# Weight unpacking, carried gate columns and half of the score mask moved from VectorE to ScalarE and GpSimd in a chunked delta-rule attention with a gated MoE

## The chip, the cores and the metric

The kernel runs on one core of one Trainium2 chip. A core has five engines that each run their own instructions in order and meet through semaphores: TensorE (PE, with its weight loads as PEld), VectorE (DVE), ScalarE (ACT), GpSimd (POOL) and SyncE (SP, which here only starts transfers). The metric is the device time of one launch in microseconds, lower is better. A change is given as the median of several runs against runs of the kernel before.

## What is computed

An attention with a decaying state, corrected by a delta rule, over 768 tokens, for 4 batches and 8 heads of width 40; then its output (4, 768, 320) goes through a linear layer to 1024 columns, a convolution of three tokens per column, a sigmoid gate and a linear layer back to 320.

```python
for t in range(S):                      # attention, state (B, H, 40, 40)
    y[:, :, t] = einsum('bhd,bhde->bhe', rt, state)
    Sa = einsum('bhde,bhe->bhd', state, at)
    state = state * wt - einsum('bhd,bhe->bhde', Sa, bt) + einsum('bhd,bhe->bhde', vt, kt)
...
h = maximum(x @ w_in, 0)                # x: (B, S, 320)
conv_out[s] = conv_w[0] * h[s-1] + conv_w[1] * h[s] + conv_w[2] * h[s+1]
out = (h / (1 + exp(-conv_out))) @ w_out
```

The inputs come as 64-bit floats; the attention's inputs are converted ahead, the three weight arrays are read by the kernel as pairs of 32-bit words.

## The kernel before

**Attention.** The 768 tokens are 24 chunks of 32. Within a chunk the recurrence is a triangular system, so that a chunk needs one inverse, and the state (four tiles of 120x360, one per batch) moves once per chunk. Two chunks make a pair j (12 pairs). Per pair: `decays` and `decayed` (scans and products with the decay, on DVE), `scores` (L421 to L440: products of the decayed rows on PE into a bank `ps` of 128x512, half for k and half for b, masked by a strict triangle on DVE into `at`), `solve_in` (the b half of `at` goes out to memory and back, turned, as `bb`), `solve` (L469: 31 steps of two operations each, L480 and L486, then the result goes out and back as `tt`). The inverse of even pairs is worked out on DVE and that of odd pairs on POOL (`VSOL`). Per chunk: `chain` (L505: `psb` on ACT, `pu` on PE from `tt` and `psb`, `u` on ACT, then the new state `pn` on PE, an addition L562 on DVE, four products with the decay L568 on POOL), the turns (`rt`, `vt`, `ut`, `sn`: PE transposes copied by ACT), `pairs` and `outputs` (`pm`, `ms`, `py`, `ysb`) and `finish` (`xf` on DVE, and its two parts `xh` by ACT and `xl` by POOL).

**Weights.** 23 pieces: twelve of w_in (`wi<g><q>`, 120x256: g is a third of the 320 rows, q a quarter of the 1024 columns), the conv weights (`cv`, 24x128), eight of w_out (`wo0` to `wo7`, 128x256) and two with its rest (`wp0`, `wp1`). Each is loaded as 64-bit words, turned into 32-bit floats on DVE by `from_f64` (L213 to L236, eight operations), copied by ACT to the high part (L253, `wih`, `woh`), and the difference is put by POOL into the low part (L255, `wil`, `wol`). The pieces' buffers come from a pool of eight (`gh` and `gl`, four each), so that the first operation on a later piece waits until the last reader of an earlier one is through. The conv piece ends in a PE transpose `pc` (L269).

**Gate.** 12 windows of 64 tokens, each in four groups fp of two times 128 columns. `moe_in` (L687): products into a bank `ph`, relu by ACT into `hb` (L714), whose first two token columns are carried over from the window before: `he`, a part of `hend`, is copied into `hb` (L712) before the relu, and the last two columns go from `hb` to `he` (L716) after it, 128x16 elements each. Then `cc`: the middle tap on ACT (L721), the two outer taps on DVE (L729), sigmoid on ACT (L734), the gate product on DVE (L736), and the split into `g..h` (ACT, L740) and `g..l` (POOL, L743). `moe_out` multiplies by w_out.

**Order.** All work is written as generators with steps (`yield`), and the string `ORDER` says token by token which generator runs one step next: `we7` is a step of weight piece 7, `so1` a stretch of the inverse of pair 1, `ch2` a step of the chain of chunk 2, `mi0.1` one of `moe_in` of window 0, group 1. Every engine runs its instructions in the order in which the steps give them out. A step of a weight piece holds a whole `from_f64`; within `solve` a step ends at i in (4, 8, 12, 16, 20, 24, 28).

Of the kernel before, what the change touches and what calls it, by code (L numbers as in the profile page):

```python
# [8 lines left out]
F32 = mybir.dt.float32  # L9
# [3 lines left out]
AF = mybir.ActivationFunctionType  # L13
ALU = mybir.AluOpType
# [3 lines left out]
C = 32  # L18
# [94 lines left out]
def tile_decay_delta_attention_then_conv_gate_moe(  # L113
# [13 lines left out]
    nc = tc.nc  # L127
    B, H, S, D = r.shape
# [5 lines left out]
    W = WS * C  # L134
# [7 lines left out]
    cp = ctx.enter_context(tc.tile_pool(name="cp", bufs=1))  # L142
# [9 lines left out]
    def bank(shape, name):  # L152
        return psS.tile(shape, F32, tag="S", name=name)

    def buf(pool, shape, tag, name, dt=F32):
        return pool.tile(shape, dt, tag=tag, bufs=BUFS[tag], name=name)

    def quad(i):
        return slice(C * i, C * i + C)
# [7 lines left out]
        out=hmask, in_=hmask, compare_op=ALU.is_ge, fill=0.0,  # L167
# [3 lines left out]
        out=hmask, in_=hmask, compare_op=ALU.is_ge, fill=0.0,  # L171
        base=D - 1, pattern=[[D, 3]], channel_multiplier=-1,
    )
    tri = cp.tile([128, C], F32, name="tri")
    nc.gpsimd.memset(tri, 1.0)
    for q in range(B):
        nc.gpsimd.affine_select(
            out=tri[quad(q), :], in_=tri[quad(q), :],
            compare_op=ALU.is_ge, fill=0.0,
            base=-1, pattern=[[1, C]], channel_multiplier=-1,  # L180
        )
    trin = cp.tile([128, 2, 1, C], F32, name="trin")
    nc.vector.tensor_copy(trin[:, 0, 0], tri)
    nc.vector.tensor_scalar(
        out=trin[:, 1, 0], in0=tri, scalar1=-1.0, scalar2=None, op0=ALU.mult
    )
    xini = cp.tile([128, HS, C], BF16, name="xini")
    nc.gpsimd.memset(xini, 1.0)
    for z in range(2):
        zs = slice(z * 64, z * 64 + 64)  # L190
        nc.gpsimd.affine_select(
            out=xini[zs], in_=xini[zs], compare_op=ALU.is_equal, fill=0.0,
# [20 lines left out]
    def from_f64(raw, e, t, m):  # L213

        lo, hi = raw[..., 0], raw[..., 1]
        V = nc.vector
        V.tensor_scalar(
            out=e, in0=hi, scalar1=20, scalar2=0x7FF,
            op0=ALU.logical_shift_right, op1=ALU.bitwise_and,
        )  # L220
        V.tensor_scalar(
            out=t, in0=hi, scalar1=3, scalar2=0x3FFFFFFF,
            op0=ALU.logical_shift_left, op1=ALU.bitwise_and,
        )
        V.scalar_tensor_tensor(
            out=t, in0=hi, scalar=-(1 << 30), in1=t, op0=ALU.bitwise_and, op1=ALU.bitwise_or
        )
        V.tensor_scalar(out=m, in0=lo, scalar1=8, scalar2=None, op0=ALU.logical_shift_right)
        tf, ef = t.bitcast(F32), e.bitcast(F32)
        V.scalar_tensor_tensor(out=tf, in0=e, scalar=896.5, in1=tf, op0=ALU.is_ge, op1=ALU.mult)  # L230
        V.tensor_scalar(out=e, in0=t, scalar1=-(1 << 23), scalar2=None, op0=ALU.bitwise_and)
        V.scalar_tensor_tensor(
            out=ef, in0=m, scalar=2.0**-44, in1=ef, op0=ALU.mult, op1=ALU.mult
        )
        V.tensor_tensor(tf, tf, ef, ALU.add)
        return tf  # L236

    def words(nm):
# [5 lines left out]
    def piece(nm, load, dsth, dstl, rows, shape):  # L244
        raw, e, t, m = words(nm)
        raw = raw[:rows]
        load(raw)
        yield
        f = from_f64(raw.rearrange("p (c z) -> p c z", z=2), e[:rows], t[:rows], m[:rows])
        if len(shape) == 2:  # L250
            f = f.rearrange("p (a c) -> p a c", a=shape[0])
        yield
        nc.scalar.copy(dsth, f)  # L253
        yield
        nc.gpsimd.tensor_tensor(dstl, f, dsth.bitcast(F32), ALU.subtract)  # L255
        yield

    def conv_piece():
        NCV = KW * NF
        craw, ce, ct, cm = words("cv")  # L260
        nc.sync.dma_start(craw[:NCV, :256], conv_w.rearrange("k (f p) -> (k f) p", p=256))
        yield
        cf = from_f64(
            craw[:NCV, :256].rearrange("p (c z) -> p c z", z=2),
            ce[:NCV, :128], ct[:NCV, :128], cm[:NCV, :128],
        )
        yield
        pc = psM.tile([128, 512], F32, tag="M", name="pc")
        nc.tensor.transpose(pc[:, :NCV], cf, ident[:NCV, :NCV])  # L269
        nc.scalar.copy(cw.rearrange("p k f -> p (k f)"), pc[:, :NCV])  # L270
        yield
        yield
# [132 lines left out]
    def against(ps, x, lhs, mk, first):  # L405

        for g in range(G):
            lo, hi = GH[g]
            h0 = (0, 3, 6)[g]
            for bi in range(B):  # L410
                nc.tensor.matmul(
                    ps[quad(bi), x, h0 : h0 + hi - lo, :], lhs[:, g, quad(bi)],
                    mk[:, g, lo:hi, quad(bi)],
                    start=(first and g == 0), stop=True, skip_group_check=True,
                )

    def gbt(t):
        return t.rearrange("p g b t -> p g (b t)")


    def scores(st):  # L421
        n, c, pd = st["n"], st["c"], st["pd"]
        ah = gbt(pd["ah"][:, c])
        ap = buf(wn, [GR, G, 3, BC], "ap", f"ap{n}")
        for h in range(3):
            g1 = 2 if h == 0 else 3
            nc.scalar.activation(  # L427
                out=ap[:, :g1, h, :], in_=ah[:, :g1], func=AF.Copy, scale=hmask[:, h : h + 1]
            )
        yield  # L430
        if c == 0:
            pd["at"] = buf(wn, [128, 2, 2, H, C], "at", f"at{n}")
        at = pd["at"]
        ps = bank([128, 2, H, C], f"ps{n}")
        for x, nm in enumerate("kb"):
            against(ps, x, gbt(pd[nm + "t"][:, c]), ap, x == 0)
        nc.vector.tensor_tensor(
            at[:, c], ps, trin.to_broadcast([128, 2, H, C]), ALU.mult,
        )
        yield  # L440

# [245 lines left out]
    def moe_in(wd, fp):  # L687
        wi, n = wd["n"], wd["n"]
        xh, xl, xp = wd["xh"], wd["xl"], wd["xp"]
        passes = (  # L690
            (wih[:, 0], xh[:, 0]), (wih[:, 1], xh[:, 1]), (wih[:, 2], xh[:, 2]),
            (wil[:, 0], xh[:, 0]), (wih[:, 0], xl[:, 0]), (wih[:, 1], xl[:, 1]),
            (wil[:, 1], xp), (wil[:, 2], xl[:, 2]),
        )
        ph = psM.tile([128, FP, B, W], F32, tag="M", name=f"ph{n}{fp}")
        for j in range(FP):
            f = FP * fp + j
            fs = slice(f * 128, (f + 1) * 128)
            for i, (l, x) in enumerate(passes):
                nc.tensor.matmul(  # L700
                    ph[:, j], l[:, fs], x,
                    start=(j == 0 and i == 0), stop=(i == len(passes) - 1),
                    skip_group_check=True,
                )
            if j == 0:
                yield
                hb = buf(mo, [128, FP, B, W + 2], "hb", f"hb{n}{fp}")
                he = hend[:, FP * fp : FP * fp + FP]
                if wi == 0:
                    nc.gpsimd.memset(hb[:, :, :, 0:2], 0.0)  # L710
                else:
                    nc.vector.tensor_copy(hb[:, :, :, 0:2], he)  # L712
                yield
        nc.scalar.activation(out=hb[:, :, :, 2 : W + 2], in_=ph, func=AF.Relu)  # L714
        yield
        nc.vector.tensor_copy(he, hb[:, :, :, W : W + 2])  # L716
        yield
        cc = buf(mo, [128, FP, B, W], "cc", f"cc{n}{fp}")
        for j in range(FP):
            f = FP * fp + j  # L720
            nc.scalar.activation(  # L721
                out=cc[:, j], in_=hb[:, j, :, 1 : W + 1], func=AF.Copy,
                scale=cw[:, 1, f : f + 1],
            )
        yield
        for j in range(FP):
            f = FP * fp + j
            for x in (0, 2):
                nc.vector.scalar_tensor_tensor(  # L729
                    out=cc[:, j], in0=hb[:, j, :, x : W + x], scalar=cw[:, x, f : f + 1],  # L730
                    in1=cc[:, j], op0=ALU.mult, op1=ALU.add,
                )
        yield
        nc.scalar.activation(out=cc, in_=cc, func=AF.Sigmoid)  # L734
        yield
        nc.vector.tensor_tensor(cc, cc, hb[:, :, :, 1 : W + 1], ALU.mult)  # L736
        yield
        c2 = cc.rearrange("p j b t -> p (j b t)")
        gh = gp.tile([128, 512], F32R, tag="gh", name=f"g{n}{fp}h")
        nc.scalar.copy(gh, c2)  # L740
        yield
        gl = gp.tile([128, 512], F32R, tag="gl", name=f"g{n}{fp}l")
        nc.gpsimd.tensor_tensor(gl, c2, gh.bitcast(F32), ALU.subtract)  # L743
        wd["gs"][fp] = [t.rearrange("p (j b t) -> p j b t", j=FP, b=B) for t in (gh, gl)]
        yield
# [137 lines left out]
    for st in sts:  # L883
        n, j, c = st["n"], st["n"] // 2, st["c"]
# [118 lines left out]
```

## Time and profile before

| | |
|---|---|
| median of 3 runs | 711.65 us (707.79 to 715.09) |
| the profiled execution | 708.08 us, of it 706.4 span |
| mean granted TensorE clock | 0.906 |
| PE busy | 560.7 us, 79% of the span |
| DVE busy | 538.4 us, 76% |
| ACT busy | 350.7 us, 50% |
| POOL busy | 353.2 us, 50% |

The table's lower part is the first part of the profile page; the span is the time from the first to the last instruction, and 1.7 us of the profiled execution lie around it. Busy shares over the whole span mix two stages: up to some 200 us weights and the first six or seven chunks, after that chunks and windows together. In the rows below, a name such as `wi12q` is the tile of that piece, an L number is the line of the kernel before, an arrow in brackets names what the engine waited for; "x23" counts instructions.

### The profile page before, as it was taken

The page shows a single profiled execution, that of the slowest core. Times are in us where ns is not written, and L with a number is a line of the kernel's source. Part 1 is how long each engine was busy: PE and PEld are TensorE (multiplying, and loading weights), DVE is VectorE, ACT ScalarE, POOL GpSimd, SP SyncE. Part 2 cuts the span into 40 slices and gives each one's busy share as a digit, 9 for nine tenths or more (in the row PEclk, how much of TensorE's full clock was granted, in tenths as well). Part 3 has the DMA queues.
Part 4 walks back from the last instruction along what each step waited for, and adds up shares of the span by engine and source line. Part 5 has one row for each costly group of instructions (what it writes and reads, how often), then busy time and mean ns, then how long its engine had stood idle before and what let it go on. Part 6 is the DMA issues. An engine that isn't in the chain of part 4 may idle for free. (4 is left out here: it accounts for less than half of the span.)

```text
span 706.4 us, 29930 instructions
## 1 busy us (share of the span) xinstructions
PE 560.7 (79%) x13021; PEld 497.9 (70%) x13021; DVE 538.4 (76%) x1261; ACT 350.7 (50%) x792; POOL 353.2 (50%) x582
## 2 busy tenths in 40 slices
PE   4444764677687898988977996899998977899886
PEld 3334654566576787977866885789887876788775
DVE  6689889998999896657795578987979894456571
ACT  2322244254375455664454664466565546455651
POOL 2001884037786235783234884236985028863321
PEclk9766777997799998989999998999998999999998
DMA  8765456437125344544404446524435025121000
GB/s 139 120 117 108 103 112 102 95 94 144 22 41 107 56 72 79 94 81 82 82 20 89 86 86 106 81 60 69 89 62 91 6 54 94 29 51 32 21 30 19
DMA packets 242402, 53.40 MB, mean 76 GB/s; under 512 B 229000, under 2 KB 238112, under 8 KB 242272
## 3 DMA queue, kind: packets, MB, share of 16 engines
q1 hardware_dynamic: 242272, 51.50, 39.9%
q8 instruction: 102, 1.67, 1.0%
q14 instruction: 28, 0.23, 0.1%
HBM read 38.63 MB, written 10.22 MB: 69 GB/s over the span
## 5 line engine op out<-in xcount | busy, mean ns | idle before, releaser
L729 DVE SCALAR_TENSOR_TENSOR cc<-hb,cw,cc 128x256 f32<-128x256 f32 x192 | 106.3, 575 | 13.7 <-ACT cc L721 10.2
L568 POOL TENSOR_TENSOR s<-s,wc 120x360 f32<-120x360 f32 x88 | 75.8, 891 | 69.4 <-DVE s L562 69.4
L486 POOL TENSOR_TENSOR xx<-xx,st 128x126 f32<-128x126 f32 (+22 forms) x186 | 83.1, 447 | 14.6
L480 POOL TENSOR_TENSOR st<-xx,bb 128x126 f32<-128x126 f32 (+22 forms) x186 | 79.4, 427 | 21.1 <-DMA bb<-bd 8.4
L700 PE MATMUL ph<-xh,wih 120*128 120x256 f32 x288 | 56.6, 306 | 11.3 <-ACT hb L714 11.3
L486 DVE TENSOR_TENSOR xx<-xx,st 128x126 f32<-128x126 f32 (+22 forms) x186 | 54.2, 291 | 6.4
L480 DVE TENSOR_TENSOR st<-xx,bb 128x126 f32<-128x126 f32 (+22 forms) x186 | 53.6, 288 | 7.2 <-DMA bb<-bd 1.7
L736 DVE TENSOR_TENSOR cc<-cc,hb 128x512 f32<-128x512 f32 x48 | 40.8, 857 | 21.7 <-ACT cc L734 21.5
L562 DVE TENSOR_TENSOR s<-pn,s 120x360 f32<-120x360 f32 x88 | 40.6, 522 | 20.6 <-PE pn L549 20.6
L700 PEld LDWEIGHTS ph<-xh,wih 120*128 120x128 f32 x288 | 41.8, 194 | 15.0 <-ACT hb L714 13.1
L734 ACT ACTIVATE cc<-cc 128x512 f32<-128x512 f32 x48 | 30.4, 636 | 43.6 <-DVE cc L729 43.5
L667 POOL TENSOR_TENSOR xl<-xf,xh 120x384 fp32r<-120x384 f32 x24 | 26.8, 1117 | 45.2 <-ACT xh L665 41.5
L721 ACT ACTIVATE cc<-hb,cw 128x256 f32<-128x256 f32 x96 | 43.5, 506 | 8.7 <-DVE hb L712 2.9
L602 PE MATMUL pt<-ident,s 120*120 120x120 f32 x276 | 40.6, 279 | 6.4 <-DVE s L562 3.2
L427 ACT ACTIVATE ap<-ah,hmask 120x384 f32<-120x384 f32 (+1 forms) x72 | 36.6, 576 | 17.4 <-DVE ah L391 10.1
L604 ACT COPY sn<-pt 120x360 f32<-120x360 f32 x92 | 38.9, 471 | 12.2 <-PE pt L602 11.8
L714 ACT ACTIVATE hb<-ph 128x512 f32<-128x512 f32 x48 | 28.8, 600 | 27.2 <-PE ph L700 23.4
L579 ACT ACTIVATE rp<-pr,hmask 120x384 f32<-120x384 f32 x72 | 36.7, 586 | 6.9 <-PE pr L576 6.5
L700 PE MATMUL ph<-xl,wih 120*128 120x256 f32 x192 | 39.3, 287 | 0.0
L533 PE MATMUL pu<-psb,tt 32*32 32x40 f32 x1536 | 22.5, 209 | 19.6 <-ACT psb L527 16.1
L602 PEld LDWEIGHTS pt<-ident,s 120*120 120x120 f32 x276 | 31.2, 143 | 9.0 <-DVE s L562 3.5
L533 PEld LDWEIGHTS pu<-psb,tt 32*32 32x32 f32 x1536 | 18.7, 114 | 24.5 <-ACT psb L527 17.7
(867 smaller groups left out, 1665.9 us busy)
## 6 DMA issues: line engine op xcount, KB each, us to landing
bb<-bd SPq DMA_DIRECT2D x24, 256.0 KB
w<-in_w_dram SPq DMA_DIRECT2D x24, 160.0 KB
a<-in_a_dram SPq DMA_DIRECT2D x24, 160.0 KB
k<-in_k_dram SPq DMA_DIRECT2D x24, 160.0 KB
b<-in_b_dram SPq DMA_DIRECT2D x24, 160.0 KB
r<-in_r_dram SPq DMA_DIRECT2D x96, 40.0 KB
v<-in_v_dram SPq DMA_DIRECT2D x96, 40.0 KB
out_dram<-ob SPq DMA_DIRECT2D x22, 160.0 KB
```

Source lines behind the costliest of these rows:

```text
L480: eng.tensor_tensor(t3, xx[:, 0:nj, i : i + 1].to_broadcast([128, nj, nt]), bb[:, i : i + 1, i + 1 :].to_broadcast([128, nj, nt]), ALU.mult,)
L486: eng.tensor_tensor(xx[:, 0:nj, i + 1 :], xx[:, 0:nj, i + 1 :], t3, ALU.add)
L533: nc.tensor.matmul(pu[quad(bi), hc], tt[quad(bi), c, h, :], psb[quad(bi), hc], start=(h == 0), stop=True, skip_group_check=True,)
L562: nc.vector.tensor_tensor(new, pn[bi][:GR], old[bi], ALU.add)
L568: nc.gpsimd.tensor_tensor(n4, n4, w4, ALU.mult)
L579: nc.scalar.activation(out=rp[:, :, h, :], in_=pr[:GR], func=AF.Copy, scale=hmask[:, h : h + 1])
L602: nc.tensor.transpose(pt[:GR, g, :], old[bi][:, g, :], ident[:GR, :GR])
L604: nc.scalar.copy(sn, pt[:GR])
L700: nc.tensor.matmul(ph[:, j], l[:, fs], x, start=(j == 0 and i == 0), stop=(i == len(passes) - 1), skip_group_check=True,)
L721: nc.scalar.activation(out=cc[:, j], in_=hb[:, j, :, 1 : W + 1], func=AF.Copy, scale=cw[:, 1, f : f + 1],)
L729: nc.vector.scalar_tensor_tensor(out=cc[:, j], in0=hb[:, j, :, x : W + x], scalar=cw[:, x, f : f + 1], in1=cc[:, j], op0=ALU.mult, op1=ALU ...
L736: nc.vector.tensor_tensor(cc, cc, hb[:, :, :, 1 : W + 1], ALU.mult)
```

## The change

Three edits; the order table and the engines of the inverses stay.

1. `from_f64`: the scaling of the low word by 2^-44 becomes an operation of its own on ACT (integer read, float written in place); the multiplication with the exponent and the final addition go to POOL. Before, these were two operations on DVE (one did scaling and multiplication together).
2. `scores`: the b half of the bank is no longer masked, only negated, by ACT (the inverse reads of it only what lies beyond the triangle); the k half is masked on DVE with `tri`. The tile `trin` and the two operations that set it up go.
3. `moe_in`: both copies of the carried columns go to ACT.

```diff
-    trin = cp.tile([128, 2, 1, C], F32, name="trin")
-    nc.vector.tensor_copy(trin[:, 0, 0], tri)
-    nc.vector.tensor_scalar(
-        out=trin[:, 1, 0], in0=tri, scalar1=-1.0, scalar2=None, op0=ALU.mult
-    )
...
         tf, ef = t.bitcast(F32), e.bitcast(F32)
+        nc.scalar.activation(out=m.bitcast(F32), in_=m, func=AF.Copy, scale=2.0**-44)
         V.scalar_tensor_tensor(out=tf, in0=e, scalar=896.5, in1=tf, op0=ALU.is_ge, op1=ALU.mult)
         V.tensor_scalar(out=e, in0=t, scalar1=-(1 << 23), scalar2=None, op0=ALU.bitwise_and)
-        V.scalar_tensor_tensor(
-            out=ef, in0=m, scalar=2.0**-44, in1=ef, op0=ALU.mult, op1=ALU.mult
-        )
-        V.tensor_tensor(tf, tf, ef, ALU.add)
+        nc.gpsimd.tensor_tensor(ef, m.bitcast(F32), ef, ALU.mult)
+        nc.gpsimd.tensor_tensor(tf, tf, ef, ALU.add)
...
+        nc.scalar.activation(out=at[:, c, 1], in_=ps[:, 1], func=AF.Copy, scale=-1.0)
         nc.vector.tensor_tensor(
-            at[:, c], ps, trin.to_broadcast([128, 2, H, C]), ALU.mult,
+            at[:, c, 0], ps[:, 0], tri.unsqueeze(1).to_broadcast([128, H, C]), ALU.mult,
         )
...
-                    nc.vector.tensor_copy(hb[:, :, :, 0:2], he)
+                    nc.scalar.copy(hb[:, :, :, 0:2], he)
...
-        nc.vector.tensor_copy(he, hb[:, :, :, W : W + 2])
+        nc.scalar.copy(he, hb[:, :, :, W : W + 2])
```

Line numbers shift: L253 and L255 become L247 and L249, L480 and L486 become L475 and L481, L538 becomes L533, L644 becomes L639; the new lines are L225 (the scaling on ACT), L228 and L229 (the two operations on POOL), L431 (the negated half on ACT) and L707 and L711 (the carried columns on ACT). Per piece DVE has six operations where it had eight, ACT two where it had one, POOL three where it had one. PE's and SP's instructions keep their order.

Where the new instructions stand is set by the steps. On ACT, in the stretch where the pieces of w_in are unpacked beside the chain of chunk 1 (`psb_1073` and `u_1123` before are `psb_1081` and `u_1132` now; a number behind an underscore only counts tiles), before:

```order
L644 COPY ysb_992<-py_927 128x320
L527 ACTIVATE psb_1073<-pp_1028 128x320
L253 CAST wih<-wi02q 120x256
L253 CAST wih<-wi12q 120x256
L538 COPY u_1123<-pu_1090 128x320
```

and now:

```order
L639 COPY ysb_999<-py_934 128x320
L225 ACTIVATE wi02s<-wi02s 120x256
L522 ACTIVATE psb_1081<-pp_1036 128x320
L247 CAST wih<-wi02q 120x256
L225 ACTIVATE wi12s<-wi12s 120x256
L247 CAST wih<-wi12q 120x256
L533 COPY u_1132<-pu_1099 128x320
```

The scaling of the pieces wi02 and wi12 (`wi02s`, `wi12s`) stands ahead of their casts, and the cast of wi12 stands ahead of the copy `u` as it did.

On POOL, inside the inverse of pair 1 (`xx_821` before, `xx_828` now), from the step that ends with i = 19 on, before:

```order
L480 TENSOR_TENSOR st_19_1165<-xx_821,bb_673 128x120
L486 TENSOR_TENSOR xx_821<-xx_821,st_19_1165 128x10x12
L255 TENSOR_TENSOR wil<-wi22q,wih 120x256
L480 TENSOR_TENSOR st_20_1398<-xx_821,bb_673 128x121
L486 TENSOR_TENSOR xx_821<-xx_821,st_20_1398 128x11x11
```

and now:

```order
L481 TENSOR_TENSOR xx_828<-xx_828,st_19_1174 128x10x12
L228 TENSOR_TENSOR wi22q<-wi22s,wi22q 120x256
L229 TENSOR_TENSOR wi22q<-wi22q 120x256
L249 TENSOR_TENSOR wil<-wi22q,wih 120x256
L228 TENSOR_TENSOR wi03q<-wi03s,wi03q 120x256
L229 TENSOR_TENSOR wi03q<-wi03q 120x256
L228 TENSOR_TENSOR wi13q<-wi13s,wi13q 120x256
L229 TENSOR_TENSOR wi13q<-wi13q 120x256
L475 TENSOR_TENSOR st_20_1410<-xx_828,bb_680 128x121
L481 TENSOR_TENSOR xx_828<-xx_828,st_20_1410 128x11x11
```

The multiplications and additions of wi22, wi03 and wi13 stand between two steps of the inverse, where only one subtraction stood. The scaling of wi13 that the last of them needs stands on ACT here, before:

```order
L644 COPY ysb_1376<-py_1299 128x320
L451 COPY khat_1378<-pz4k 128x320
L665 CAST xh_1002<-xf_1008 120x12x32
L593 COPY vt_1436<-pvt_1432 120x384
L253 CAST wih<-wi13q 120x256
```

and now, behind the copies `ysb` and `khat`:

```order
L639 COPY ysb_1387<-py_1310 128x320
L446 COPY khat_1389<-pz4k 128x320
L225 ACTIVATE wi13s<-wi13s 120x256
L660 CAST xh_1010<-xf_1016 120x12x32
L588 COPY vt_1448<-pvt_1444 120x384
L247 CAST wih<-wi13q 120x256
```

The scaling came in behind `khat`; the casts of wi13 and wi03 are behind it in the old order.

Later on POOL, inside the inverse of pair 3 (`xx_2479` before, `xx_2502` now), where wo5 was subtracted, before:

```order
L480 TENSOR_TENSOR st_7_2730<-xx_2479,bb_2475 128x96
L486 TENSOR_TENSOR xx_2479<-xx_2479,st_7_2730 128x4x24
L255 TENSOR_TENSOR wol<-wo5q,woh 128x256
L480 TENSOR_TENSOR st_8_2814<-xx_2479,bb_2475 128x115
L486 TENSOR_TENSOR xx_2479<-xx_2479,st_8_2814 128x5x23
```

and now:

```order
L475 TENSOR_TENSOR st_7_2755<-xx_2502,bb_2498 128x96
L481 TENSOR_TENSOR xx_2502<-xx_2502,st_7_2755 128x4x24
L249 TENSOR_TENSOR wol<-wo5q,woh 128x256
L228 TENSOR_TENSOR wo7q<-wo7s,wo7q 128x256
L229 TENSOR_TENSOR wo7q<-wo7q 128x256
L475 TENSOR_TENSOR st_8_2840<-xx_2502,bb_2498 128x115
L481 TENSOR_TENSOR xx_2502<-xx_2502,st_8_2840 128x5x23
```

The pair of wo7 now stands between the subtraction of wo5 and the steps of the inverse from i = 8 on; the subtraction of wo7 stays where it was, behind the step i = 15.

## The prediction

> **What bounds the kernel now.** I read the view of stages first, since the change has two halves: 21 of the 23 weight pieces are worked on between 50 and 200 us (the count in the row of L232 below), the gate's columns almost all after that. Columns: PE, PEld, DVE, ACT and POOL busy, then granted clock.
>
> ```profile
> 50.00:100.00 50.00, 30.85 (x876) 26.19 (x878) 45.11 (x112) 15.66 (x39) 28.62 (x58) 0.70 0.53 103
> 100.00:150.00 50.00, 31.59 (x843) 27.39 (x834) 44.64 (x125) 21.98 (x51) 18.02 (x30) 0.84 0.48 98
> 150.00:200.00 50.00, 37.35 (x991) 32.21 (x992) 45.96 (x101) 21.40 (x51) 33.09 (x58) 0.80 0.38 75
> ...
> 235.00:706.00 471.00, 412.04 (x9488) 370.23 (x9488) 335.29 (x763) 256.46 (x576) 246.67 (x384) 0.95 0.35 63
> ```
>
> From 50 to 200 us DVE is busy 90% (135.7 of 150 us) and PE 67%; after 235 us PE is busy 87% (412 of 471). So freed DVE time can be worth its full length early, and little late. But POOL, which takes the work, is not idle evenly. Its own lines, through the second triangular solve (L480 and L486, pair 1, on POOL), with the weight subtractions L255 that already stand in it:
>
> ```profile
> 71.08 0.24 POOL L480 TENSOR_TENSOR st<-xx,bb 128x31 f32<-128x31 f32 x1 [5.59 <-DMA bb<-bd]
> ...
> 82.74 0.91 POOL L255 TENSOR_TENSOR wil<-wi21q,wih 120x256 fp32r<-120x256 f32 x1
> 83.61 0.41 POOL L480 TENSOR_TENSOR st<-xx,bb 128x133 f32<-128x133 f32 x1
> ...
> 87.94 0.78 POOL L255 TENSOR_TENSOR wil<-wi12q,wih 120x256 fp32r<-120x256 f32 x1
> ...
> 93.91 0.78 POOL L255 TENSOR_TENSOR wil<-wi22q,wih 120x256 fp32r<-120x256 f32 x1
> ...
> 105.68 1.00 POOL L667 TENSOR_TENSOR xl<-xf,xh 120x384 fp32r<-120x384 f32 x1
> ```
>
> No row between 71.08 and 105.68 shows idle time: this solve is as long as POOL's work in it, 34.6 us. What comes out of it, the inverse of pair 1, is needed by the state chain of chunk 2. The view of waits has POOL's rest elsewhere, in one piece of 23 us among others, which lies behind that solve:
>
> ```profile
> POOL s L568 <- DVE s L562: 69.4, 13, 23.4
> ```
>
> **The change part by part.** Gone from DVE:
>
> ```profile
> 50.00:200.00 150.00, 10.05 (x21) 0.78 0.46 92
> ...
> 50.00:200.00 150.00, 9.46 (x21) 0.78 0.46 92
> ...
> L437 DVE TENSOR_TENSOR at<-ps,trin x24: 671/682/693, 17.8 to 576.5; 128x512 f32<-128x512 f32 x24
> ...
> L712 DVE COPY hb<-hend 128x16 f32<-128x16 f32 x44 | 12.6, 289 | 0.3
> L716 DVE COPY hend<-hb 128x16 f32<-128x16 f32 x48 | 12.4, 264 | 16.6 <-ACT hb L714 16.5
> ...
> L716 DVE COPY hend<-hb x48: 160/171/960, 148.0 to 686.8; 128x16 f32<-128x16 f32 x48
> ```
>
> The first two rows are the multiplication L232 and the addition L235: 19.5 us over 21 pieces, 0.93 us a piece, on the engine that bounds 50 to 200 us. The mask product L437 halves; a copy of 16 columns takes 0.16 us, 512 take 0.68, so 256 take by a straight line 0.41, 0.27 us less a chunk (between 0 and half, 0.34). The carried columns free 25.0 us, nearly all after 148 us. The two set-up operations on the mask run at 3 us, ahead of the first transfers the solves wait for: nothing.
>
> Prices of what is added, by the nearest rows: on POOL 0.78 to 0.91 us for each of 46 two-input operations (the L255 rows above, same shape: 1.7 us a piece); on ACT, by these rows,
>
> ```profile
> L253 ACT CAST wih<-wi10q x1: 405/405/405, 30.4 to 30.4; 120x256 fp32r<-120x256 f32 x1
> ...
> L270 ACT COPY cw<-pc x1: 178/178/178, 118.3 to 118.3; 128x24 f32<-128x24 f32 x1
> ...
> L451 ACT COPY khat<-pz0k x1: 426/426/426, 22.2 to 22.2; 128x320 f32<-128x320 f32 x1
> ```
>
> 0.4 us for the scaling m of a piece, 0.43 us for the negated half of the scores, 0.18 us for each of 92 column copies.
>
> *Solve of pair 1.* The changed order puts ten of the new POOL operations inside it, those of wi02, wi12, wi22, wi03 and wi13, and ACT's casts of these pieces, in a fixed order with the state chain's copies, now wait for them. The ACT rows concerned:
>
> ```profile
> 86.17 0.41 ACT L253 CAST wih<-wi12q 120x256 fp32r<-120x256 f32 x1 [4.53 <-DVE wi12q L235]
> 86.48 0.42 ACT L538 COPY u<-pu 128x320 f32<-128x320 f32 x1
> ...
> 92.18 0.41 ACT L253 CAST wih<-wi22q 120x256 fp32r<-120x256 f32 x1 [3.15 <-DVE wi22q L235]
> 92.49 1.52 ACT L579 ACTIVATE rp<-pr,hmask 120x384 f32<-120x384 f32 x3
> ...
> 100.83 0.42 ACT L644 COPY ysb<-py 128x320 f32<-128x320 f32 x1 [5.36 <-PE py L638]
> ```
>
> POOL reaches the end of wi12's addition after wi02's pair, four steps of the solve and its own pair: 87.94 + 1.7 + 1.7 = 91.3. The cast moves from 86.17 to 91.3, and u of chunk 1 behind it by 5. Two subtractions and four steps (93.91 − 87.94 = 6.0) and wi22's pair later it is 99.4 with the cast's own 0.4: the cast of wi22 moves by 7.2, so do rp, the products behind it and ysb, to about 108.0. ACT's scaling of wi13 stands behind ysb and one more copy (0.84 us): done near 109.3. POOL, which has finished wi03 by 102.3, idles for it 7 us, does wi13 by 111.0, and only then the last eleven steps (105.68 − 94.69 = 11.0): the solve ends at 122, against 105.7, **16 us late**: 8.5 of new work, 7 of waiting.
>
> Behind it stand one split, the subtraction of wi13, the four state products, that of wi03, a split, wi23 and the conv weights. The new wait for buffers binds here too: DVE's first operations on the conv piece wait until wi13 and wi03 have been subtracted, with the piece wo0 and the next pair's decayed inputs queued behind them. SP's loads of later pieces wait for DVE's reading of the raw words, as before, and move with DVE.
>
> ```profile
> 111.65 0.87 POOL L255 TENSOR_TENSOR wil<-wi03q,wih 120x256 fp32r<-120x256 f32 x1
> 112.49 1.03 POOL L667 TENSOR_TENSOR xl<-xf,xh 120x384 fp32r<-120x384 f32 x1
> ...
> 117.96 0.30 PE L269 MATMUL pc<-ident,cvq 24*128 24x24 f32 x1 [7.85 <-DVE cvq L235]
> ```
>
> wi03 was subtracted by 112.5 and will be at 129, the conv piece is ready at 132, where PE, which already waited 7.85 us for it, had it at 117.96: **14 us late for PE and all in line behind it**. POOL's 23 us of rest comes only after this and is no cover.
>
> *Pieces wo2 to wo7.* Here DVE sets the pace and gives back 0.93 us a piece. The rows of the solve of pair 3, on POOL again:
>
> ```profile
> 165.63 0.24 POOL L480 TENSOR_TENSOR st<-xx,bb 128x31 f32<-128x31 f32 x1 [1.10 <-DMA bb<-bd]
> ...
> 174.82 1.03 POOL L480 TENSOR_TENSOR st<-xx,bb 128x115 f32<-128x115 f32 x1
> ...
> 193.20 0.85 POOL L255 TENSOR_TENSOR wol<-wo6q,woh 128x256 fp32r<-128x256 f32 x1 [3.27 <-ACT woh L253]
> ...
> 215.77 1.02 POOL L667 TENSOR_TENSOR xl<-xf,xh 120x384 fp32r<-120x384 f32 x1
> ...
> 187.43 0.43 DVE L231 TENSOR_SCALAR wo7q<-wo7q 128x256 int32<-128x256 int32 x1
> ...
> 220.54 2.83 SPq L496 DMA_DIRECT2D tt<-xd  x4
> ...
> 231.50 0.79 PE L533 MATMUL pu<-psb,tt 32*32 32x40 f32 x64 [1.78 <-ACT psb L527]
> ```
>
> The new POOL pair of wo7 stands where POOL was at 174.82, but DVE gives it its input only at 187.86: even with nothing late before, POOL waits 13 us, less the 4 that DVE has saved. With DVE late by 9 (14 less five pieces) to 14, I take 12 since casts and copies also hold this stage: 199.9, 0.4 for ACT's scaling and 1.7 for the pair give 202.0, 27 us behind. Two more pieces add 3.4, and the old rest of 3.27 us absorbs as much: the solve ends at 243 where it ended at 215.8. Its result goes out and comes back (issued at 220.54) and is used at 231.50; the two are at most 8 us apart once the issue has run, and the flight has to fit in, so I take 6 of slack: **chunk 6 starts 21 us late**.
>
> *After 235 us* DVE has nearly all of the 25 us and about half of the 24 half masks (3 us) less, ACT 92 × 0.18 + 12 × 0.43 = 22 us more, on 54% busy (256 of 471). PE's idle time that the gate's copies can touch:
>
> ```profile
> PE ph L700 <- ACT hb L714: 11.3, 9, 4.5
> ```
>
> All of it gone would be −11; all small copies on the path +17. ACT has more room than DVE had, so I take −4. PE's order does not change, and what had run ahead of it while the chunks were late saves perhaps 2 more.
>
> Sum: 708.1 (profiled execution: 706.4 span and 1.7 around it) + 21 − 4 − 2 = 723. The median of the runs shown, 711.65, lies 3.6 higher: **727 us** for a median run.
>
> How POOL shares its way to memory with DVE is the open cost. Two DVE operations, each alone and beside POOL's work:
>
> ```profile
> L228 DVE TENSOR_SCALAR wi01s<-wi01r x1: 284/284/284, 58.4 to 58.4; 120x256 int32<-120x256 int32 x1
> L228 DVE TENSOR_SCALAR wi11s<-wi11r x1: 815/815/815, 61.0 to 61.0; 120x256 int32<-120x256 int32 x1
> ...
> L232 DVE SCALAR_TENSOR_TENSOR wi00q<-wi00s,wi00q x1: 425/425/425, 16.8 to 16.8; 120x256 f32<-120x256 int32 x1
> ...
> 84.99 0.58 DVE L232 SCALAR_TENSOR_TENSOR wi12q<-wi12s,wi12q 120x256 f32<-120x256 int32 x1
> ```
>
> L228 lost 0.53 us, L232 inside the solve of pair 1 only 0.16, and 46 new POOL operations beside DVE would cost between nothing and 46 × 0.53 = 24 us. I take nothing beyond the sum, since in the two solves DVE will mostly be waiting; the upper end is a rival. The Trainium skill, page "SBUF — State Buffer", section "SBUF: two separate sides", says that the port pair these two engines share is an exclusive lock, held for a whole instruction, with the loser blocked. L228 agrees with that, L232 only in part; by that rule alone the sum would go towards 727 + 24, by the smaller loss to 727 + 7.
>
> **The rivals.**
> *Faster.* DVE bounds 50 to 200 us, its 19.5 us come back in full, and POOL has room for its share. Then 711.65 − 19.5 = 692, or up to 704 if some is lost. It holds if u of chunk 1 (ACT, 86.48) does not come later than before. Against it: POOL has no gap from 71.08 to 105.68. 0.16.
> *No change.* The first delay arises but DVE's relief takes back 10 of 14, and POOL's wait for wo7 fits in later rests: +4 − 6, 705 to 718. Against it: solve 3 too is dense on POOL. 0.16.
> *Larger loss by the shared port*, or both delays in full and nothing won after 235: 738 to 751. 0.12.
>
> **How the numbers follow.** The likeliest course, both solves late, gets 0.56 and gives the predicted time, 727, with 719 to 738 as its own range. Slower altogether 0.56 + 0.12 = 0.68. A measurement of this kernel tells about 1% (7 us) from no change. The range leaves out the faster rival and the top of the largest loss, 0.2 together: 705 to 745.
>
> **What would show it.** Right: the solve of pair 1 on POOL lasts about 50 us instead of 34.6, with a wait for ACT's scaling of wi13 in it; PE's conv transpose near 132; POOL waiting over 8 us for DVE or ACT at wo7; chunk 6's pu near 252. Wrong: POOL's new operations at under 0.5 us; the conv transpose at 118 or before; DVE's busy share from 50 to 200 us falling while the 235 us mark of before is reached earlier.

## The result and the profile after

| | before | changed |
|---|---|---|
| median | 710.18 us (707.79 to 715.09, 4 runs) | 735.12 us (731.12 to 738.58, 4 runs) |
| ratio, 95% interval | | 1.0366 [1.0319, 1.0412] |
| profiled execution's span | 706.4 us | 731.6 us |
| DVE busy | 538.4 us | 500.0 us |
| ACT, POOL busy | 350.7, 353.2 us | 375.6, 383.3 us |

The kernel became 25 us slower while VectorE was relieved of 38 us. The view of stages of the changed kernel (columns as before; the last row is the same late work, again 471 us, that ran from 235 to 706 us before):

```profile
50.00:100.00 50.00, 25.04 (x682) 21.18 (x678) 36.02 (x84) 16.62 (x43) 34.93 (x62) 0.70 0.47 92
100.00:150.00 50.00, 27.50 (x693) 23.44 (x689) 35.22 (x89) 18.39 (x46) 25.49 (x44) 0.67 0.45 86
150.00:200.00 50.00, 36.73 (x879) 32.22 (x870) 35.63 (x85) 23.00 (x56) 25.82 (x44) 0.84 0.47 97
...
260.00:731.00 471.00, 410.56 (x9568) 369.42 (x9554) 318.70 (x684) 270.23 (x675) 246.63 (x384) 0.96 0.35 64
```

From 50 to 200 us VectorE is busy 71% now, where it was 90%: it no longer bounds this stage, it waits in it. TensorE did 89.3 us of work there instead of 99.8; what it did not do came later. In the last 471 us the two kernels run alike (TensorE 411 and 412 us).

The same places as in the prediction, on POOL (start, duration, and in brackets the idle time before it with its releaser): the solve of pair 1, then what stood behind it, then the solve of pair 3.

```profile
69.62 0.24 POOL L475 TENSOR_TENSOR st<-xx,bb 128x31 f32<-128x31 f32 x1 [1.90 <-DMA bb<-bd]
...
95.53 0.90 POOL L228 TENSOR_TENSOR wi22q<-wi22s,wi22q 120x256 f32<-120x256 f32 x1
96.51 0.98 POOL L229 TENSOR_TENSOR wi22q<-wi22q 120x256 f32<-120x256 f32 x1
...
100.11 0.73 POOL L228 TENSOR_TENSOR wi03q<-wi03s,wi03q 120x256 f32<-120x256 f32 x1 [1.38 <-ACT wi03s L225]
...
106.30 0.73 POOL L228 TENSOR_TENSOR wi13q<-wi13s,wi13q 120x256 f32<-120x256 f32 x1 [4.66 <-ACT wi13s L225]
...
119.56 0.99 POOL L662 TENSOR_TENSOR xl<-xf,xh 120x384 fp32r<-120x384 f32 x1
120.51 0.72 POOL L249 TENSOR_TENSOR wil<-wi13q,wih 120x256 fp32r<-120x256 f32 x1
121.19 3.10 POOL L563 TENSOR_TENSOR s<-s,wc 120x360 f32<-120x360 f32 x4
124.26 0.72 POOL L249 TENSOR_TENSOR wil<-wi03q,wih 120x256 fp32r<-120x256 f32 x1
...
128.28 0.51 POOL L229 TENSOR_TENSOR cvq<-cvq 24x128 f32<-24x128 f32 x1
...
203.65 0.72 POOL L228 TENSOR_TENSOR wo7q<-wo7s,wo7q 128x256 f32<-128x256 f32 x1 [7.01 <-DVE wo7q L227]
...
209.45 3.05 POOL L563 TENSOR_TENSOR s<-s,wc 120x360 f32<-120x360 f32 x4
...
243.52 1.01 POOL L662 TENSOR_TENSOR xl<-xf,xh 120x384 fp32r<-120x384 f32 x1
```

The solve of pair 1 lasts from 69.62 to 119.56, 49.9 us where it took 34.6. Two of its gaps are in these rows, 1.38 and 4.66 us, both for ScalarE's scaling. The other two are 0.52 us each. The pair of wo7 waits 7.01 us for VectorE, and the solve of pair 3 ends at 243.5 where it ended at 215.8. VectorE's and TensorE's side of the conv piece:

```profile
121.27 0.79 DVE L212 TENSOR_SCALAR cvq<-cvr 24x128 int32<-24x128 int32 x1 [3.05 <-POOL wil L249]
...
125.01 0.99 DVE L223 TENSOR_SCALAR cvs<-cvr 24x128 int32<-24x128 int32 x1 [1.37 <-POOL wil L249]
...
128.85 0.30 PE L263 MATMUL pc<-ident,cvq 24*128 24x24 f32 x1 [5.20 <-POOL cvq L229]
```

VectorE's first operation on the conv piece starts when the subtraction of wi13 has ended (120.51 + 0.72), the fourth when that of wi03 has (124.26 + 0.72), and TensorE's transpose comes at 128.85 instead of 117.96.

To see where time is lost I compare the start of ACT's copy `psb` for one chunk in two kernels. Before it stands at 127.33 (chunk 2), 166.95 (4), 189.78 (5), 231.04 (6) and 647.27 us (23). How much later it is, and in the column pc how much later TensorE's conv transpose is (117.96 us before):

| kernel | pc | chunk 2 | chunk 4 | chunk 5 | chunk 6 | chunk 23 |
|---|---|---|---|---|---|---|
| changed | +10.9 | +12.0 | +14.9 | +25.3 | +28.0 | +24.8 |
| mask and columns only (e1) | −0.6 | −0.8 | −0.2 | −1.7 | −0.9 | −5.5 |
| weights only (e2) | +11.3 | +11.8 | +14.2 | +26.0 | +27.6 | +28.2 |
| first five back (e3) | −1.0 | +0.2 | +3.8 | +14.9 | +18.1 | +16.7 |
| last five back (e4) | +12.3 | +12.8 | +15.9 | +14.6 | +16.2 | +11.4 |
| ten back (e5) | +0.1 | +1.3 | +4.7 | +4.0 | +4.8 | +1.2 |
| pairs with cast (e6) | +11.8 | +12.6 | +13.7 | +21.9 | +26.2 | +20.1 |
| subtraction three times (e7) | +9.1 | +9.3 | +11.6 | +14.6 | +19.2 | +22.7 |
| columns only (e8) | −1.1 | −1.1 | −0.9 | −1.4 | −1.4 | −4.6 |
| wo7 back (e9) | +11.2 | +12.4 | +15.7 | +19.6 | +22.9 | +19.2 |
| wi03, wi13 back (e10) | +3.9 | +5.0 | +8.7 | +19.7 | +23.0 | +21.7 |
| products 1 on DVE (e11) | +10.0 | +10.9 | +14.4 | +24.8 | +28.9 | +26.8 |
| products 1 and 4 on DVE (e12) | +11.1 | +11.5 | +14.2 | +19.3 | +25.2 | +22.4 |

Each row is one execution. Up to chunk 2 the changed kernel, e2, e4 and e9 have the same weight edit, and they lie within 1 us of each other there. Later the granted clock adds to the spread: between chunks 5 and 6 TensorE was busy 33.7 us at a clock of 0.94 before and 38.7 us at 0.84 in e12. At chunk 23 a few us tell nothing: the four runs of the changed kernel alone lie between 731.12 and 738.58 us.

The changed kernel loses 12 us up to chunk 2, 3 between chunks 2 and 4, another 10 between chunks 4 and 5 and 3 up to chunk 6. The 3 us that it seems to win between chunks 6 and 23 are not clear of the noise.

### The profile page after: what moved, and what is told of

It is laid out like the page before. It is cut to its first block, busy times and chain, and to the rows that moved or that the text cites. A ratio compares the mean times of both kernels' runs of the same rounds, so it can differ in the third digit from the quotient of the medians.

```text
span 731.6 us, 29925 instructions
## 1 busy us (share of the span) xinstructions
PE 565.0 (77%) x13021; PEld 501.3 (69%) x13021; DVE 500.0 (68%) x1121; ACT 375.6 (51%) x931; POOL 383.3 (52%) x628
## 5 line engine op out<-in xcount | busy, mean ns | idle before, releaser
L724 DVE SCALAR_TENSOR_TENSOR cc<-hb,cw,cc 128x256 f32<-128x256 f32 x192 | 105.3, 570 | 29.6 <-ACT cc L716 26.2
L563 POOL TENSOR_TENSOR s<-s,wc 120x360 f32<-120x360 f32 x88 | 74.2, 873 | 55.6 <-DVE s L557 55.6
L481 POOL TENSOR_TENSOR xx<-xx,st 128x126 f32<-128x126 f32 (+22 forms) x186 | 80.9, 435 | 14.6
L475 POOL TENSOR_TENSOR st<-xx,bb 128x126 f32<-128x126 f32 (+22 forms) x186 | 77.7, 418 | 17.2 <-DMA bb<-bd 4.4
L695 PE MATMUL ph<-xh,wih 120*128 120x256 f32 x288 | 57.0, 308 | 12.1 <-ACT hb L709 12.1
L481 DVE TENSOR_TENSOR xx<-xx,st 128x126 f32<-128x126 f32 (+22 forms) x186 | 56.3, 302 | 6.4
L475 DVE TENSOR_TENSOR st<-xx,bb 128x126 f32<-128x126 f32 (+22 forms) x186 | 53.6, 288 | 6.7 <-DMA bb<-bd 0.9
L695 PEld LDWEIGHTS ph<-xh,wih 120*128 120x128 f32 x288 | 42.0, 195 | 17.3 <-ACT hb L709 13.9
L574 ACT ACTIVATE rp<-pr,hmask 120x384 f32<-120x384 f32 x72 | 36.7, 585 | 6.6 <-PE pr L571 6.0
L528 PE MATMUL pu<-psb,tt 32*32 32x40 f32 x1536 | 22.9, 210 | 18.1 <-ACT psb L522 16.2
L544 PE MATMUL pn<-v,khat 32*120 32x120 f32 x552 | 28.5, 310 | 9.9 <-ACT u L533 4.7
```

The source lines that it names most:

```text
L475: eng.tensor_tensor(t3, xx[:, 0:nj, i : i + 1].to_broadcast([128, nj, nt]), bb[:, i : i + 1, i + 1 :].to_broadcast([128, nj, nt]), ALU.mult,)
L481: eng.tensor_tensor(xx[:, 0:nj, i + 1 :], xx[:, 0:nj, i + 1 :], t3, ALU.add)
L563: nc.gpsimd.tensor_tensor(n4, n4, w4, ALU.mult)
L574: nc.scalar.activation(out=rp[:, :, h, :], in_=pr[:GR], func=AF.Copy, scale=hmask[:, h : h + 1])
L695: nc.tensor.matmul(ph[:, j], l[:, fs], x, start=(j == 0 and i == 0), stop=(i == len(passes) - 1), skip_group_check=True,)
L724: nc.vector.scalar_tensor_tensor(out=cc[:, j], in0=hb[:, j, :, x : W + x], scalar=cw[:, x, f : f + 1], in1=cc[:, j], op0=ALU.mult, op1=ALU ...
```

## The experiments

Theory A is the prediction's: the weight operations on GpSimd stand in its solves and ahead of what the chain needs, in two places. Rival B is a price for every GpSimd operation, wherever it stands, through the way to memory that the prediction has it share with VectorE. Rival C is that the small copies on ScalarE cost something late. Each kernel was run beside the kernel before; ratios carry 95% intervals.

**Which of the three edits.** e1 puts all eight operations of `from_f64` back on VectorE in the changed kernel, e2 makes only the weight edit in the kernel before, e8 only the carried columns.

```diff
 # e1, against the changed kernel
-        nc.scalar.activation(out=m.bitcast(F32), in_=m, func=AF.Copy, scale=2.0**-44)
...
-        nc.gpsimd.tensor_tensor(ef, m.bitcast(F32), ef, ALU.mult)
-        nc.gpsimd.tensor_tensor(tf, tf, ef, ALU.add)
+        V.scalar_tensor_tensor(
+            out=ef, in0=m, scalar=2.0**-44, in1=ef, op0=ALU.mult, op1=ALU.mult
+        )
+        V.tensor_tensor(tf, tf, ef, ALU.add)
```

> The changed kernel with from_f64 wholly back on VectorE; the negated half of the mask and the carried columns stay on ScalarE. Theory A (the weight operations on GpSimd stand in its two triangular solves and in front of what the state chain waits for; they are the whole loss): the changed kernel lost 28 us by chunk 6 and won 3 us after it, so this one should be 3 us faster than before, 704 to 709 us against 710. Rival C (the small copies on ScalarE delay the gate, and the weights only hide it): slower than before, above 715 us.

Measured: 707.58 us against 709.61, 0.9956 [0.9916, 0.9997].

> The kernel before with the weight edit alone. Theory A: the delay of 25 to 28 us at chunk 6 stays and nothing is won after it: 735 to 740 us. Rival C: less than 728 us, since the copies on ScalarE are missing.

Measured: 735.06 us, 1.0349 [1.0274, 1.0423].

> The kernel before with the carried columns alone on ScalarE. It takes 25 us of VectorE's and adds 19 to ScalarE's after 200 us. Theory A (TensorE bounds that stage): 705 to 710 us, at most 4 us won. A rival (VectorE's time counts there too): 695 to 702 us.

```diff
 # e8, against the kernel before
-                    nc.vector.tensor_copy(hb[:, :, :, 0:2], he)
+                    nc.scalar.copy(hb[:, :, :, 0:2], he)
...
-        nc.vector.tensor_copy(he, hb[:, :, :, W : W + 2])
+        nc.scalar.copy(he, hb[:, :, :, W : W + 2])
```

Measured: 708.65 us against 711.97, 0.9960 [0.9913, 1.0007]. The loss is the weight edit's alone; C falls. Mask and columns together win about as much as the columns alone, at most 1%, and beside the weight edit nothing that can be told (e2 735.06 us, the changed kernel 735.12). That they take some 30 us from VectorE shows how little VectorE's time is worth after 200 us, where most of them lie.

**Which pieces.** e3 leaves the pieces of the solve of pair 1 on VectorE, e4 those of the solve of pair 3, e5 both groups; the other pieces stay on GpSimd.

```diff
 # e3, e4, e5 (and e9, e10), against the changed kernel
+OWN = ("wi02", "wi12", "wi22", "wi03", "wi13",)
...
+        if own:
+            V.scalar_tensor_tensor(
+                out=ef, in0=m, scalar=2.0**-44, in1=ef, op0=ALU.mult, op1=ALU.mult
+            )
+            V.tensor_tensor(tf, tf, ef, ALU.add)
+        else:
+            nc.gpsimd.tensor_tensor(ef, m.bitcast(F32), ef, ALU.mult)
+            nc.gpsimd.tensor_tensor(tf, tf, ef, ALU.add)
```

> The changed kernel with the multiplication and addition of wi02, wi12, wi22, wi03 and wi13 back on VectorE, those whose operations stood in the solve of pair 1; 18 pieces stay on GpSimd. Theory A: the solve of pair 1 lasts 35 us as before instead of 50, psb of chunk 2 is at most 4 us late instead of 12, the second delay at wo7 stays with 10 to 16: 719 to 726 us. Rival B (every GpSimd operation costs the same by the port that it shares with VectorE, 25 us over 23 pieces): 5 of 23 pieces back give 5 us, 730 us.

Measured: 723.73 us, 1.0196 [1.0126, 1.0266]; chunk 2 is 0.2 us late.

> The changed kernel with wo5, wo6, wo7, wp0 and wp1 back on VectorE, those whose operations stood in the solve of pair 3. Theory A: psb of chunk 2 is 12 us late as in the changed kernel, and no more is added up to chunk 6, 3 us come back after it: 717 to 723 us. Rival B: 5 of 23 pieces back, 730 us.

Measured: 722.65 us, 1.0176 [1.0101, 1.0250]; chunk 2 is 12.8 us late, and 3.4 us are added up to chunk 6, where the changed kernel adds 16. That was not expected; 3.1 of it arise between chunks 2 and 4, as in the changed kernel.

> The changed kernel with both groups back on VectorE, wi02, wi12, wi22, wi03, wi13 and wo5, wo6, wo7, wp0, wp1; 13 pieces stay on GpSimd, outside its two solves. Theory A: each group alone took back 11 to 12 us, and they lie one behind the other, so both give 23 to 27 and the rest costs nothing: 708 to 714 us. If the 13 pieces that stay delay the chain in places of their own, or VectorE's old load comes back as a limit: 715 to 720 us.

Measured: 711.10 us against 711.97, 1.0019 [0.9977, 1.0061]. Five pieces of 23 are worth nearly half of the loss each time, and the two halves add up. B, as one price for each operation, falls: it would leave 13 of 23 parts of the loss, some 14 us. But the 13 pieces outside the solves are not free. The right measure for them is e1, which has the same mask and columns and leaves the unpacking wholly on VectorE: 0.9956 against 1.0019 here, 0.6% or some 4 us, at the edge of what the two intervals can tell. The traces say the same: at chunk 6 e5 is 5.7 us behind e1. Between chunks 2 and 4 every kernel with the weight edit loses 1.1 to 3.6 us, e1 and e8 0.6 and 0.2. What carries this third, smaller delay was not followed.

**Work or waits?** A has both in the solves: 8.5 us of new operations and 7 of waits for pair 1. e6 gives the two GpSimd operations out just ahead of ScalarE's cast, which takes those of wi03 and wi13 out of the solve and brings those of wi21 into it. e7 leaves the kernel before as it was, but makes the old subtraction three times.

```diff
 # e6, against the changed kernel
-        nc.gpsimd.tensor_tensor(ef, m.bitcast(F32), ef, ALU.mult)
-        nc.gpsimd.tensor_tensor(tf, tf, ef, ALU.add)
-        return tf
+
+        def rest():
+            nc.gpsimd.tensor_tensor(ef, m.bitcast(F32), ef, ALU.mult)
+            nc.gpsimd.tensor_tensor(tf, tf, ef, ALU.add)
+
+        return tf, rest
...
+        rest()
         nc.scalar.copy(dsth, f)
 # e7, against the kernel before
-        nc.gpsimd.tensor_tensor(dstl, f, dsth.bitcast(F32), ALU.subtract)
+        for _ in range(3):
+            nc.gpsimd.tensor_tensor(dstl, f, dsth.bitcast(F32), ALU.subtract)
```

> The changed kernel, where GpSimd's multiplication and addition of a piece are given out in the step of ScalarE's cast, just ahead of it, instead of in VectorE's step. The pairs of wi03 and wi13 then stand behind the solve of pair 1, so that its wait for ScalarE's scaling of wi13 is gone; the pairs of wi02, wi12, wi22 and of wo7 stay inside the solves. If the waits inside the solves carry the loss: the solve of pair 1 lasts 40 us instead of 50, psb of chunk 2 is 5 to 8 us late, the wait at wo7 stays: 722 to 730 us. If it is the work on GpSimd wherever it stands: 733 to 737 us.

Measured: 731.33 us, 1.0345 [1.0278, 1.0412], hardly to be told from the changed kernel and between the two values expected. POOL in e6, behind the solve of pair 1:

```profile
112.30 0.72 POOL L230 TENSOR_TENSOR wi13q<-wi13s,wi13q 120x256 f32<-120x256 f32 x1
...
119.92 1.37 POOL L253 TENSOR_TENSOR wil<-wi03q,wih 120x256 fp32r<-120x256 f32 x1
...
128.99 0.72 POOL L231 TENSOR_TENSOR cvq<-cvq 24x128 f32<-24x128 f32 x1
```

The solve ends at 112.3 instead of 119.6, as expected, but nothing behind it comes earlier: the two pairs now stand between the solve and the subtractions, and the conv piece is added at 128.99, even 0.7 us later than in the changed kernel. My estimate of 722 to 730 us followed the solve's end and forgot that the line behind it had grown by as much. Nor did the waits go: those of 1.38 and 4.66 us are gone, but others came into the line (0.83 us in the solve, 1.19, 1.82 and 0.52 behind it), so that 5.4 us of waits stand up to the conv piece where the changed kernel has 7.3. So e6 moves work and waits and does not tell them apart.

> The kernel before, where GpSimd makes each piece's subtraction three times: 44 more operations of the same size on GpSimd as in the change (the conv piece has none), in places of old ones, with no new wait for another engine. If the work of the new operations carries the loss: 722 to 730 us, the solve of pair 1 6 us longer and the state chain behind it. If the new waits carry it: 710 to 716 us.

Measured: 729.98 us, 1.0302 [1.0227, 1.0376]. That is the value for work, not for waits: 44 operations cost about 20 us, though GpSimd has no new wait for another engine. VectorE in e7 at the conv piece:

```profile
118.06 0.79 DVE L217 TENSOR_SCALAR cvq<-cvr 24x128 int32<-24x128 int32 x1 [2.21 <-POOL wil L256]
...
123.39 0.99 DVE L228 TENSOR_SCALAR cvs<-cvr 24x128 int32<-24x128 int32 x1 [2.97 <-POOL wil L256]
```

The buffer wait that was slack before binds here as in the changed kernel. GpSimd's line from the start of the solve of pair 1 to the conv piece is thus a chain of its own with hardly any slack.

e7 is not the change without its waits, though: from the start of that solve up to the last subtraction of wi03 it has 12 new operations, the changed kernel 10. It shows that work alone can cost this much, not what the waits cost in the changed kernel. There the rows say: some 8 us of work and 7.1 of waits make the solve of 34.6 us one of 49.9; of these 15.3 us, 13.9 are left at its end since it began 1.5 earlier, 12.5 at the subtraction of wi03, and 10.9 at the transpose.

**Through what does the first delay reach the chain?** The prediction named the conv piece. But TensorE also waited 7.80 us in the changed kernel for the four state products of chunk 1, which stand in the same line (121.19 above):

```profile
122.04 1.61 PE L597 MATMUL pt<-ident,s 120*120 120x120 f32 x6 [7.80 <-POOL s L563]
```

e11 puts these on VectorE.

```diff
 # e11 (n == 1) and e12 (n in (1, 4)), against the changed kernel
-                nc.gpsimd.tensor_tensor(n4, n4, w4, ALU.mult)
+                (nc.vector if n == 1 else nc.gpsimd).tensor_tensor(n4, n4, w4, ALU.mult)
```

> The changed kernel with the four state products of chunk 1 on VectorE instead of GpSimd, where they stood behind the solve of pair 1; TensorE waited 7.8 us for them. If these products carry the first delay to the chain: psb of chunk 2 is 3 to 7 us late instead of 12, the time 726 to 731 us. If the conv piece carries it, as the prediction had it (VectorE's wait for the buffers of wi13 and wi03, TensorE's conv transpose): psb stays 10 to 12 us late, 733 to 736 us.

Measured: 735.05 us, 1.0373 [1.0323, 1.0423]; chunk 2 is 10.9 us late. VectorE and TensorE in e11:

```profile
123.02 0.72 DVE L212 TENSOR_SCALAR cvq<-cvr 24x128 int32<-24x128 int32 x1 [2.37 <-POOL wil L249]
...
127.92 0.29 PE L263 MATMUL pc<-ident,cvq 24*128 24x24 f32 x1 [11.84 <-POOL cvq L229]
```

TensorE's wait for the products is gone and has moved to the conv transpose: 11.84 us, where it waited 7.80 and 5.20. VectorE still waits there for the subtraction of wi13. So the conv piece holds the first delay by itself. The products alone would have given much of it too; that is argued from the 7.80 us and was not run.

> The changed kernel with the pairs of wi03 and wi13 alone back on VectorE. They are 4 of the operations inside the solve of pair 1 and hold all but 1 us of its waits (1.4 and 4.7 us). If work and waits both count: that solve ends 4 us late instead of 14, psb of chunk 2 5 us late instead of 12, the time 726 to 729 us. If the waits there are covered by others, as the run with the pairs ahead of the cast says, only 3 us of work go: 731 to 734 us.

Measured: 728.87 us, 1.0298 [1.0264, 1.0333]. With wi03 and wi13 back on VectorE the solve of pair 1 ends 3 us late and chunk 2 starts 5.0 us late instead of 12.0: here 3 us of work and 6 of waits went together, and 7 came back. Waits inside the solve count when nothing takes their place in the line behind it. By chunk 6 only 5 of the 7 are left; the other 2 go in three steps of 0.6 to 0.8 us, each no larger than the spread of such rows.

**The second delay.** TensorE's first product with the state for chunk 5, before and changed:

```profile
184.04 0.76 PE L514 MATMUL pp<-s,ah 120*32 120x120 f32 x24
...
210.29 0.61 PE L509 MATMUL pp<-s,ah 120*32 120x120 f32 x2 [8.70 <-POOL s L563]
```

It waited for nothing before; now it waits 8.70 us for the state products of chunk 4, which stand in the solve of pair 3 behind the pair of wo7 (209.45 above).

> The changed kernel with the pair of wo7 alone back on VectorE. In the changed kernel GpSimd waits 7.0 us for VectorE at this pair inside the solve of pair 3, with the state products of chunk 4 behind it. If this wait carries the second delay: psb of chunk 5 is 16 to 18 us late instead of 25, the time 725 to 729 us. If only the work counts (2 of 10 operations inside this solve): 732 to 735 us.

Measured: 726.16 us, 1.0249 [1.0208, 1.0289]. One piece out of 23 is worth 8 to 9 us. POOL no longer waits there, and chunk 5 is 19.6 us late instead of 25.3. I had expected 16 to 18; 4 us still arise between chunks 4 and 5, and that these are the work of wo5 and wo6 in the same solve is likely and was not tried.

> As the run before it, and the four state products of chunk 4 on VectorE too, which stood in the solve of pair 3 behind the pair of wo7. If they carry the second delay: psb of chunk 5 is less than 5 us later than psb of chunk 4 by the comparison with the kernel before (it was 10 in the changed kernel), the time 8 us or more under the run before it. If the solve's own end carries it, chunk 6 is as late as there: the two runs within 3 us.

Measured: 731.45 us, 1.0333 [1.0284, 1.0382]. Chunk 5 is 19.3 us late instead of 24.8 (e11), 5.2 later than chunk 4 by the comparison, instead of 10.4; so having the products of chunk 4 on GpSimd, four steps behind wo7's pair, carried half of that. They are still late on VectorE (203.50 us, against 180.08 on GpSimd before), and TensorE still waits 3.61 us for them. Chunk 6 wins 3.7 and the whole 3.6, between the two values expected: with the products out of the way something else is nearly as late. VectorE, ScalarE and TensorE in e12:

```profile
215.41 0.81 DVE L212 TENSOR_SCALAR wp1q<-wp1r 128x256 int32<-128x256 int32 x1 [6.58 <-POOL wol L249]
...
218.05 0.42 ACT L225 ACTIVATE wp1s<-wp1s 128x256 f32<-128x256 int32 x1 [4.90 <-DVE wp1s L223]
218.37 0.41 ACT L639 COPY ysb<-py 128x320 f32<-128x320 f32 x1
...
218.83 1.18 PE L544 MATMUL pn<-v,khat 32*120 32x120 f32 x6 [1.91 <-ACT ysb L639]
...
256.75 0.79 PE L528 MATMUL pu<-psb,tt 32*32 32x40 f32 x64 [0.88 <-ACT psb L522]
```

It is a buffer wait again, one that the prediction does not have: VectorE's work on wp1 waits until GpSimd has subtracted wo6, ScalarE's new scaling of wp1 waits for VectorE, and the copy `ysb` that TensorE needs stands behind that scaling. The changed kernel has the same wait of VectorE, 12.6 us long; before there was none. The end of the solve of pair 3 (23.9 us late in e12) is not what came last: TensorE's `pu` of chunk 6, the first to need its result, waited for `psb`.

## Why the prediction was right

727 us with a range of 705 to 745 was forecast, 735.1 came; 17 us more than before were forecast, 25 came. The two places named are where most of the time is lost, and the way of the first delay is the one forecast. The way of the second was not, and the terms of the sum show it: +28 at chunk 6 where 21 stood, −3 after it where −6 stood, 1.8 us from the profiled execution to the median where 3.6 stood. Point by point:

- *Prices.* POOL's 46 operations took 0.80 us in the mean (36.7 us), ScalarE's scalings 0.41, its halves of the scores 0.39 and its column copies 0.21 (forecast 0.78 to 0.91, 0.4, 0.43, 0.18); VectorE's half mask 0.42 (forecast 0.41).
- *Solve of pair 1.* It lasted 49.9 us, forecast about 50; it ended 13.9 us late (forecast 16), mainly because it began 1.5 us earlier. Its waits are 7.1 us in sum, forecast 7, and the largest is for the scaling of wi13, as said.
- *Conv piece.* 10.9 us late, forecast 14, by the buffers' way that was forecast; e11 shows that this way is the one that holds. The size was off since the state products took 3.1 us, where the rows before had 4.4, and the solve began earlier.
- *Wo7.* POOL waited 7.0 us (forecast over 8); the solve of pair 3 ended at 243.5, forecast 243. That hit is partly luck: wo7's pair ended at 205.3 instead of 202.0, and the rest of the solve took 38.2 us instead of 41.
- *Chunk 6.* 28 us late, forecast 21; its `pu` at 259.5, forecast near 252. This is the step that failed. "I take 6 of slack" looked at the way from the solve's end through memory to chunk 6. The delay came by another way and one chunk earlier: the state products of chunk 4 stand in the same solve on POOL, 29.4 us late (209.45 against 180.08), and TensorE, which needs them for chunk 5, waited 8.70 us for them (chunk 5 +25.3). e9 and e12 show it: without wo7's wait, or with the products elsewhere, chunk 5 is 5.5 to 5.7 us earlier.
- *After 235 us.* −3 (chunk 6 to 23) where −6 was in the sum, and e2, which has none of the late edits, is as fast as the changed kernel. TensorE waits for the relu as before:

```profile
PE ph L695 <- ACT hb L709: 12.1, 9, 5.4
```

11.3 us before, 12.1 now: the third of it that was to go stayed. e1 and e8 seem to win 3 to 5 us between chunks 6 and 23, but their profiled executions (703.37 and 703.95 us) lie 4 to 5 us under their medians; by the medians each wins 0.4%, some 3 us, hardly clear of the noise. Where that comes from was not followed.
- *The rivals.* VectorE's relief on its own (0.16) fails at the point named for it: u of chunk 1 came at 89.91 instead of 86.48. No change (0.16) fails too: VectorE's relief took back nothing of the first delay, which is 10.9 us at the conv piece and 12.0 at chunk 2, and wo7's wait did not fit in later rests (e9). The larger loss by one price for each operation at the shared port (0.12) fell with e3 to e5, which leave some 4 us for the 13 pieces outside the solves. Its other half, both delays in full and nothing won after 235 us, came near: 28 us late at chunk 6 and little won after it, 735.1 us where 738 was its lower end.
- *Work and waits.* For the first solve the prediction gave 7 of 16 us to waits, and 7.1 of 15.3 came. e7 shows that work alone, with no new wait of GpSimd, costs about as much at the end; so the loss needs no waits, but e10 (7 us back for 3 of work and 6 of waits) shows that they count.

## What to carry to other kernels

An engine that is half idle over the whole span can still be without slack for the stretch that matters: look for the rows in which it runs without a gap, and for what stands behind them in its line. There, work moved to it, and waits that come with the work, cost up to their full length, and a saving on the engine that was "90% busy" only turns into waiting. Follow a late queue to every consumer behind it, not only to the result that gives it its name: here state products and buffers passed the delay on, one chunk before the solve's result was needed.

## What the runs showed of the hardware

VectorE's one-input operations on the conv piece (24x128) took 0.21 us each at 115.51, 115.64 and 116.09 before, and 0.70 to 0.99 us in the changed kernel and in e7, where a GpSimd operation ran at the same time. A short operation of VectorE beside a long one of GpSimd thus lost 0.5 to 0.8 us, up to more than the 0.53 of the row in the prediction. The first row is of the kernel before, the other two of the changed kernel:

```profile
115.51 0.21 DVE L217 TENSOR_SCALAR cvq<-cvr 24x128 int32<-24x128 int32 x1
...
124.94 0.99 POOL L662 TENSOR_TENSOR xl<-xf,xh 120x384 fp32r<-120x384 f32 x1
125.01 0.99 DVE L223 TENSOR_SCALAR cvs<-cvr 24x128 int32<-24x128 int32 x1 [1.37 <-POOL wil L249]
```

VectorE's operation started 0.07 us after GpSimd's and ended 0.07 us after it (126.00 and 125.93 us); the other three in the changed kernel (0.79, 0.83 and 0.70 us) ended 0.08 us after the GpSimd operation beside them. So what such an operation lost here is what was left of that operation, and not a fixed price. Not every operation of VectorE shows it: in the solve of pair 1 before, the row at 84.99 in the prediction lost 0.16 us.

In this kernel the sum of such losses did not decide: 13 pieces on GpSimd outside the solves cost some 4 us in all (e5 against e1), whatever their cause.
